# Attention with normalised queries and keys, then a SoLU layer: a new order of work for the first five groups of heads

## The chip, the cores and the metric

The kernel runs on one core of a Trainium2 chip. The metric is the device time of one execution in microseconds (us), the median of several runs. Times of single instructions come from one profiled execution, whose own time is given beside them. The engines are named as the profile names them: PE is the matrix engine (PEld its weight loads), DVE the vector engine, ACT the scalar engine, POOL the general engine (GpSimd), SP the engine that issues most of the transfers. Each runs its own list of instructions in order.

## The reference

Inputs are q, k and v of shape (8, 12, 448, 64), that is 96 heads of 448 rows and 64 columns, two gains of 64 values, and the weights of a feed-forward layer.

```python
q_n, k_n = (rmsnorm(q, g_q), rmsnorm(k, g_k))      # x / sqrt(mean(x*x) + 1e-6) * g
scores = 1.0 / np.sqrt(64) * np.matmul(q_n, k_n.transpose(0, 1, 3, 2))
attn = np.exp(scores - max); attn = attn / (sum + 1e-09)
x = np.matmul(attn, v)                             # laid out as 3584 tokens x 768
h = x @ w_in                                       # 768 x 1024
solu = h * softmax(h)
out = layernorm(solu, g_ln) @ w_out                # 1024 x 768
```

All of it is in 32-bit floats.

## The kernel before

**Stages.** Attention comes first (up to some 330 us of the profile), then the first product and the SoLU and norm of the feed-forward layer, then the second product. Both products are done by a scheme of seven block products. The change touches the attention only; what follows takes its input from a DRAM buffer `xd` that the attention writes, and its instructions are not changed.

**Quads and pairs.** Attention walks over 24 quads of four heads, `for m in range(NQ)`. A quad is two pairs of heads, `a = 2m` and `b = 2m + 1`. One pair's q and k fill a tile of 128 partitions by 896 values: each 32x32 block of q or k lies so that a transpose inside 32x32 blocks turns it into `qkT`, which has two heads' 64 columns on the partitions and the 448 positions along the free axis.

**Preparing a pair.** In the order in which one needs the other:

- `squares(n)` (line 662, ACT) squares the pair's q and k.
- `row_sums(n)` (line 670, DVE) sums each group of 32 values.
- `fold_sums(m)` (lines 680 and 681, POOL) adds for a whole quad the two halves of each row, which lie on different partitions: four copies of 32 partitions by 56 values, then one addition. `fold_one(n)` (lines 690 and 691, DVE) does the same for one pair, with four copies by 28 values and an addition.
- `rsqrt_seed` (lines 700 and 701, ACT) and `rsqrt_step` (lines 707 to 710, DVE) make one over the root mean square, for whatever width they are given.
- `normalise(n)` (line 719, POOL) multiplies the pair's q and k by it.
- `qk_transpose(n)` (line 729, DVE) makes `qkT`, and `gain(n)` (line 733, ACT) multiplies its q half by the product of both gains and 1/8.

Quad 0 is loaded in another layout and prepared by functions of its own (`square_rows`, `sum_rows`, `normalise_rows`, `transpose_rows`, `take_rows`, lines 738 to 794), with PE transposes.

**Attention of a quad.** `scores(n, kc)` (line 818, PE) makes the scores of one pair for 128 keys, kc = 0 to 2, and right after it ACT takes the exponential into a tile `E` (line 808). `scores_last(m)` (line 831) makes the last 64 keys of both pairs in one tile, so a quad has seven such tiles. They come from three PSUM buffers (tag "t"), which also serve the column sums `sm`. `add(n)` (line 845, DVE) adds `E` 0 and 1 of a pair into `es`. `add_more(n)` (line 854) adds `E` 2 to it, on POOL, or on DVE in the last two quads, for pairs of which `whole(n)` is true. `values_last` and `values` (lines 864 and 875, PE) multiply by v. `sums(m)` (line 897, PE) adds up the columns by products with ones: one term for the last tile, one for each `es`, and one for `E` 2 of each pair that is not whole; a term is four products, which the profile counts as eight instructions. `inverse(m)` (lines 908 to 916) takes the reciprocal, and `divide(m)` (lines 923 and 924, DVE) scales the outputs and so frees their two PSUM buffers. `store_x(m)` (line 932, SP) writes them to `xd`.

**Order.** The loop runs inside a manual schedule: each engine gets its instructions in the order in which the Python calls are made. `unit(f)` calls f and then whatever `later` has put off until that point; `later(1, divide)` at the end of a quad places `divide` after the next quad's first scores.

```python
def whole(n):
    return on_vector(n // 2) or n > 9 and n % 2 < 1
```

Quad 0 has a sequence of its own, ended by `continue`. In it each pair of quad 1 gets its own norm (`norms["one", n]`), and the squares and row sums of quad 2 follow late. From quad 1 on, `early = 3 < m and next1` separates two orders. In quads 4 to 22 (`early`) the norms of the next quad open the quad, its pair a is transposed after the first scores and pair b after the sixth. In quads 1 to 3 these calls sit at other places, a different one in each quad, and `divide` and `store_x` of quads 1 and 2 are made in the middle of the next quad's scores. `scarce = m < 5` also places `squares(b + 4)` and `add(b)` differently in quads 1 to 4.

**Loads.** `load(m)` issues eight transfers from SP (line 636). Quads 1 to 3 are loaded before the loop, quad 4 at the start of quad 1, and from then on quad m + 3 in quad m. Tiles of q and k have four buffers, those of v two.

Of the kernel before, what the change touches and what calls it, by code (L numbers as in the profile page):

```python
# [366 lines left out]
def fast_path(  # L367
# [298 lines left out]
    def row_sums(n):  # L666
        m, i = divmod(n, 2)
        if i == 0:
            norms[m] = {"part": small.tile([P, 2, 2 * NB], FP32, tag="part", name="part", bufs=2)}
        nc.vector.tensor_reduce(norms[m]["part"][:, i], st[n]["sq"], AX, OP.add)  # L670
# [9 lines left out]
            e.tensor_copy(ss[g * 32 : g * 32 + 32], part[o * 32 : o * 32 + 32])  # L680
        e.tensor_tensor(ss, ss, part, OP.add)

    def fold_one(n):

        m, i = divmod(n, 2)
        ss = small.tile([P, 4 * NB], FP32, tag="ss", name="ss", bufs=2)[:, 0 : 2 * NB]
        part = norms[m]["part"][:, i]
        for g in range(4):
            o = g ^ 1
            nc.vector.tensor_copy(ss[g * 32 : g * 32 + 32], part[o * 32 : o * 32 + 32])  # L690
        nc.vector.tensor_tensor(ss, ss, part, OP.add)
        norms["one", n] = {"ss": ss}

    def rsqrt_seed(d):
        ss = d["ss"]
        p, w = ss.shape
        y = d["y"] = small.tile([P, 4 * NB], FP32, tag="ny", name="ny", bufs=2)[0:p, 0:w]
        nc.scalar.activation(y, ss, AF.Ln, scale=1.0 / D, bias=eps[0:p])  # L700
        nc.scalar.activation(y, y, AF.Exp, scale=-0.5)

    def rsqrt_step(d):
        y, ss = d["y"], d["ss"]
        p, w = ss.shape
        x = small.tile([P, 4 * NB], FP32, tag="nx", name="nx", bufs=2)[0:p, 0:w]
        nc.vector.tensor_scalar(x, ss, -0.5 / D, -0.5e-6, OP.mult, OP.add)
        nc.vector.tensor_tensor(x, x, y, OP.mult)
        nc.vector.tensor_tensor(x, x, y, OP.mult)
        nc.vector.scalar_tensor_tensor(y, x, 1.5, y, OP.add, OP.mult)  # L710

    def normalise(n, e=nc.gpsimd):
        d = st[n]
        if ("one", n) in norms:
            y = norms["one", n]["y"]
        else:
            y = norms[n // 2]["y"][:, n % 2 * 2 * NB : (n % 2 + 1) * 2 * NB]
        d["qkn"] = work.tile([P, 2 * NB, 32], FP32, tag="qkn", name="qkn", bufs=2)
        e.tensor_tensor(  # L719
            d["qkn"].rearrange("p (s b) d -> p s b d", s=2),  # L720
            d["qk"].rearrange("p s (b d) -> p s b d", d=32),
            y.rearrange("p (s b) -> p s b ()", s=2).to_broadcast([P, 2, NB, 32]),
            OP.mult,
        )
# [6 lines left out]
    def gain(n):  # L731
        d = st[n]
        nc.scalar.activation(d["qkT"][:, 0], d["qkT"][:, 0], AF.Copy, scale=gcol[:, KF : KF + 1])
# [105 lines left out]
    def on_vector(m):  # L839
        return m >= NQ - 2  # L840

    def add(n):
        d = st[n]
        d["es"] = work.tile([P, 2, S], FP32, tag="es", name="es")
        nc.vector.tensor_tensor(d["es"], d["E", 0], d["E", 1], OP.add)  # L845

    def whole(n):
        return on_vector(n // 2) or n > 9 and n % 2 < 1

    def add_more(n):  # L850
        d = st[n]
# [518 lines left out]
    with tc.manual_schedule():  # L1370
# [19 lines left out]
        for m in range(NQ):  # L1390
            a, b = 2 * m, 2 * m + 1

            def outputs():
                values_last(m)
                values(a)


            next1 = m + 1 < NQ
            next2 = m + 2 < NQ
            next3 = m + 3 < NQ  # L1400
            if m == 0:
                unit(lambda: scores(a, 0))
                normalise_rows(1, 0)
                normalise_rows(1, 1)
                unit(lambda: scores(a, 1))
                unit(lambda: scores(a, 2))
                for s in range(2):
                    transpose_rows(1, s)
                    take_rows(1, s)
                squares(2)  # L1410
                add(a)
                row_sums(2)
                fold_one(2)
                unit(lambda: scores_last(m))
                squares(3)
                rsqrt_seed(norms["one", 2])
                rsqrt_step(norms["one", 2])
                normalise(2)
                unit(lambda: scores(b, 0))
                row_sums(3)  # L1420
                fold_one(3)
                unit(lambda: scores(b, 1))
                unit(lambda: scores(b, 2))
                rsqrt_seed(norms["one", 3])
                rsqrt_step(norms["one", 3])
                normalise(3)
                qk_transpose(2)
                gain(2)
                add(b)
                unit(outputs)  # L1430
                squares(4)
                qk_transpose(3)
                gain(3)
                unit(lambda: values(b))
                squares(5)
                unit(lambda: sums(m))
                inverse(m)
                row_sums(4)
                row_sums(5)
                fold_sums(2)  # L1440
                later(1, lambda m=m: divide(m))
                continue
            early = 3 < m and next1
            def norms_next():
                rsqrt_seed(norms[m + 1])
                rsqrt_step(norms[m + 1])
                normalise(a + 2)
                normalise(b + 2)

            if early:  # L1450
                norms_next()
            for x in joins_at.get(m, ()):
                combine_in(x)
            if next1:
                load_v(m + 1)
            if m == 1:
                load(m + 3)
            unit(lambda: scores(a, 0))
            if m not in (2, 3):
                store_x(m - 1)  # L1460
            if early:
                qk_transpose(a + 2)
                if next3:
                    load(m + 3)
            if m == 3:
                norms_next()
                divide(m - 1)
                store_x(m - 1)
            unit(lambda: scores(a, 1))
            if m == 2:  # L1470
                norms_next()
                divide(m - 1)
                store_x(m - 1)
            unit(lambda: scores(a, 2))
            if m == 3:
                qk_transpose(a + 2)
                load(m + 3)
            unit(lambda: scores_last(m))
            if m == 3:
                norm_gain()  # L1480
            if m < 2:
                add(a)
            unit(lambda: scores(b, 0))
            if m == 1:
                norms_next()
            if m == 2:
                qk_transpose(a + 2)
                load(m + 3)
            unit(lambda: scores(b, 1))
            if early or 1 < m < 4:  # L1490
                qk_transpose(b + 2)
            if m > 1:
                add(a)
                if not on_vector(m):
                    add_more(a)
            unit(lambda: scores(b, 2))
            if m == 1:
                qk_transpose(a + 2)
            scarce = m < 5
            if next2:  # L1500
                squares(a + 4)
                if not scarce:
                    squares(b + 4)
                row_sums(a + 4)
            if next1:
                gain(a + 2)
            if m == 1:
                add(b)
                qk_transpose(b + 2)
                squares(b + 4)  # L1510
            if next1:
                gain(b + 2)
            if scarce and m > 1:
                squares(b + 4)
                add(b)
            if next2:
                row_sums(b + 4)
                fold_sums(m + 2)
            if not scarce:
                add(b)  # L1520
            if on_vector(m):
                add_more(a)
                add_more(b)
            unit(outputs)
            step(m - 2)
            begin(m)
            step(m - 1)
            if m - 1 in sets:
                load_next()
            if m == 2:  # L1530
                load_next()
                load_next()
            unit(lambda: values(b))
            if m == NQ - 1:
                block_sums(0, 0)
                block_sums(0, 1)
                load_x(1)
            unit(lambda: sums(m))
            inverse(m)
            if next1 and m not in (1, 2):  # L1540
                later(1, lambda m=m: divide(m))
            if m == NQ - 2:
                load_x(0)
                sizes(0)
# [188 lines left out]
```

## Time and profile before

| what | value |
|---|---|
| runs | 809.93 us median of 3 (808.85 to 811.12) |
| the profiled execution | 809.46 us, its span 807.7 us |
| PE busy | 793.2 us, 98% of the span |
| DVE, POOL, ACT busy | 615.4, 505.7 and 474.0 us |
| chain that ended last | PE 91%, DVE 4%, ACT 1%, DMA 1%, POOL 1%, issue 1% |
| scores, values, column sums | lines 818, 875, 897 |

The span is the time from the first to the last instruction of the profiled execution; the rest of its own time lies around it. A busy share of PE of 98% does not say that nothing is to be had: matrix instructions overlap, so that small gaps hide in the sum. The chain, read in order of time, shows where PE was waiting for another engine: there it leaves PE's lines and passes through the others.

### The profile page before, as it was taken

What the parts mean: (1) busy time and instruction counts of PE and PEld (TensorE: products, weight loads), DVE (VectorE), ACT (ScalarE), POOL (GpSimd) and SP (SyncE); (2) the same over time, 40 slices, a digit from 0 to 9 for tenths busy, and PEclk for the clock granted to TensorE, in tenths of its full rate; (3) what the DMA queues carried; (4) which work ended last, traced back from release to release, by engine and by line L of the source; (5) the groups of instructions that cost most, each with busy time, mean ns of one, the idle gap of its engine ahead of it and who ended that gap; (6) DMA issues with size and microseconds to landing.
All of it is one profiled execution on the core that took longest, in us unless ns stands there. A gap on an engine that the chain in (4) does not pass through costs nothing.

```text
span 807.7 us, 14348 instructions
## 1 busy us (share of the span) xinstructions
PE 793.2 (98%) x4894; PEld 466.1 (58%) x4894; DVE 615.4 (76%) x1217; ACT 474.0 (59%) x785; POOL 505.7 (63%) x652
## 2 busy tenths in 40 slices
PE   8999999999999999999999999999899999999997
PEld 4334444444434444444444444444699999999996
DVE  6877889889888897488878667776886776866945
ACT  6677878778787774466766544453515455464420
POOL 1353677777777685234456466678487777777861
PEclk9999999999999999999999999999999999999999
DMA  9867798988877833545555445542647447365412
GB/s 164 176 149 150 166 191 191 190 180 175 172 155 165 155 97 97 139 122 153 153 135 138 110 108 144 140 116 52 209 119 256 144 176 267 117 227 192 141 60 83
DMA packets 269598, 122.68 MB, mean 152 GB/s; under 512 B 187596, under 2 KB 254668, under 8 KB 269516
## 3 DMA queue, kind: packets, MB, share of 16 engines
q1 hardware_dynamic: 254332, 111.78, 55.6%
q10 hardware_dynamic: 15184, 9.90, 4.5%
q8 instruction: 40, 0.66, 0.4%
q14 instruction: 42, 0.34, 0.1%
HBM read 84.94 MB, written 36.70 MB: 151 GB/s over the span
## 4 chain that ended last, share of the span: by engine, by line
PE 91%; DVE 4%; ACT 1%; DMA 1%; POOL 1%; issue 1%; SPq 0%; DVEq 0%; POOLq 0%; ACTq 0%
PE A L1210 15%; PE o L875 13%; PE s L818 13%; PE A L996 13%; PE B L996 8%; PE B L1210 7%; PE sm L897 5%; PE C L996 4%; PE D L996 4%; PE C L1210 4%; PE o L864 2%; PE s L831 2%; DMA ur<-ud 1%; ACT E L808 1%; DVE ub L1100 1%
## 5 line engine op out<-in xcount | busy, mean ns | idle before, releaser
L808 ACT ACTIVATE E<-s 128x896 f32<-128x896 f32 x168 | 139.1, 934 | 13.7 <-PE s L818 13.0
L818 PE MATMUL s<-qkT 64*64 64x448 f32 x1152 | 120.3, 545 | 1.4 <-ACT E L808 0.7
L875 PE MATMUL o<-E,v 128*64 128x448 f32 x576 | 113.5, 543 | 0.0
L1085 POOL TENSOR_TENSOR he<-he,mhalf 128x1 f32<-128x1 f32 x28 | 27.6, 987 | 105.4 <-DVE he L1084 104.9
L719 POOL TENSOR_TENSOR qkn<-qk,ny 128x896 f32<-128x896 f32 x46 | 77.2, 1698 | 21.1 <-DMA qk<-in_k_dram 15.1
L1210 PE MATMUL B<-w_out,sums 128*128 128x192 f32 x392 | 80.4, 328 | 2.8 <-DVE P L1272 2.1
L818 PEld LDWEIGHTS s<-qkT 64*64 64x64 f32 x1152 | 48.1, 163 | 59.3 <-ACT E L808 28.9
L1210 PE MATMUL A<-w_out,sums 128*128 128x192 f32 x392 | 80.7, 329 | 1.0 <-POOL sums L1191 0.7
L875 PEld LDWEIGHTS o<-E,v 128*64 128x64 f32 x576 | 39.2, 137 | 72.6 <-issue 67.3
L996 PE MATMUL B<-w_in,xsum 128*128 128x512 f32 x168 | 76.7, 593 | 0.4 <-POOL he L1085 0.4
L996 PE MATMUL A<-w_in,xg 128*128 128x512 f32 x168 | 74.6, 593 | 0.0
L1067 ACT ACTIVATE u<-h,hmax 128x1024 f32<-128x1024 f32 x28 | 32.1, 1148 | 62.9 <-DVE hmax L1061 62.8
L1210 PEld LDWEIGHTS B<-w_out,sums 128*128 128x128 f32 x392 | 66.8, 191 | 3.4 <-DVE P L1272 2.4
L1210 PEld LDWEIGHTS A<-w_out,sums 128*128 128x128 f32 x392 | 66.8, 191 | 1.7 <-POOL sums L1191 1.6
L680 POOL COPY ss<-part 32x56 f32<-32x56 f32 x88 | 42.0, 477 | 25.4 <-DVE part L670 21.0
L996 PEld LDWEIGHTS B<-w_in,xsum 128*128 128x128 f32 x168 | 31.8, 190 | 40.9 <-issue 38.5
L996 PEld LDWEIGHTS A<-w_in,xg 128*128 128x128 f32 x168 | 31.8, 190 | 40.1 <-issue 39.6
L854 POOL TENSOR_TENSOR es<-es,E 128x896 f32<-128x896 f32 x17 | 35.9, 2110 | 30.4 <-ACT sq L662 30.4
L845 DVE TENSOR_TENSOR es<-E 128x896 f32<-128x896 f32 x48 | 53.2, 1110 | 0.5 <-ACT E L808 0.5
L729 DVE STREAM_TRANSPOSE qkT<-qkn 128x896 f32<-128x896 f32 x46 | 48.5, 1089 | 1.8 <-POOL qkn L719 1.8
L670 DVE TENSOR_REDUCE part<-sq 128x28 f32<-128x896 f32 x46 | 48.2, 1078 | 2.2
L1210 PE MATMUL A<-w_out,s 128*128 128x192 f32 x224 | 45.6, 326 | 0.0
(152 smaller groups left out, 1658.0 us busy)
## 6 DMA issues: line engine op xcount, KB each, us to landing
ur<-ud SPq DMA_DIRECT2D x60, 256.0 KB, 4.9
ud<-ub SPq DMA_DIRECT2D x112, 128.0 KB, 2.3
xd<-xo SPq DMA_DIRECT2D x48, 224.0 KB, 3.0
qk<-in_q_dram SPq DMA_DIRECT2D x92, 112.0 KB, 3.1
qk<-in_k_dram SPq DMA_DIRECT2D x92, 112.0 KB, 3.0
v<-in_v_dram SPq DMA_DIRECT2D x24, 384.0 KB, 4.5
out_dram<-P SPq DMA_DIRECT2D x19, 384.0 KB, 4.0
raw<-in_moe_w_in_dram SPq DMA_DIRECT2D x12, 512.0 KB, 5.3
```

The costliest lines, as they stand in the source:

```text
L670: nc.vector.tensor_reduce(norms[m]["part"][:, i], st[n]["sq"], AX, OP.add)
L680: e.tensor_copy(ss[g * 32 : g * 32 + 32], part[o * 32 : o * 32 + 32])
L719: e.tensor_tensor(d["qkn"].rearrange("p (s b) d -> p s b d", s=2), d["qk"].rearrange("p s (b d) -> p s b d", d=32), y.rearrange("p (s b) - ...
L729: nc.vector.transpose(d["qkT"].rearrange("p s t -> p (s t)"), d["qkn"].rearrange("p b d -> p (b d)"))
L808: nc.scalar.activation(d["E", kc], s[:, :, 0:S], AF.Exp)
L818: nc.tensor.matmul(s[c : c + D, h, 0:S], d["qkT"][hh, 1, keys], d["qkT"][hh, 0, :], start=True, stop=True,)
L845: nc.vector.tensor_tensor(d["es"], d["E", 0], d["E", 1], OP.add)
L854: e.tensor_tensor(d["es"], d["es"], d["E", 2], OP.add)
L875: nc.tensor.matmul(d["o"][h * D : (h + 1) * D, :], quads[n // 2]["v"][:, n % 2 + 2 * h, kc], d["E", kc][:, h], start=False, stop=(kc == NJ ...
L897: nc.tensor.matmul(sm[g : g + 32, :], ones[:, w], e[:, h, t * S // 2 : (t + 1) * S // 2], start=(x == 0), stop=(x == len(terms) - 1),)
L996: nc.tensor.matmul(k[bank], a[:, c], w_in[i][:, c], start=begin and c == 0, stop=c == HD - 1, skip_group_check=not begin,)
L1210: nc.tensor.matmul(k[bank], a[:, c].rearrange("p a i -> p (a i)"), w_out[:, area, i, c], start=begin and c == 0, stop=c == KC - 1, skip_gr ...
```

## The change

Five things are done to the order of the attention, and one term of the column sums moves to POOL.

- **Quad 0.** `fold_one` is gone. The squares and row sums of pairs 2 and 3 are followed by one `fold_sums(1)` on POOL and one `norms_next()` for both pairs. `add(b)` comes earlier, ahead of those norms. `squares(4)`, `row_sums(4)` and `squares(5)` stand ahead of the transpose of pair 2, `row_sums(5)` between the two transposes, and `fold_sums(2)` after the second. `gain(3)` leaves the quad.
- **Quad 1** gets `gain(3)` after its first scores.
- **Quads 1 to 4** take the order of the later ones: norms of the next quad first, transposes after the first and the sixth scores, `add` and `squares` where the later quads have them, `divide` and `store_x` by `later` in all of them.
- **g's turn.** The transpose of the norm gain `g_ln` (`norm_gain`) in quad 3 moves from the middle of the scores to between the values of both pairs.
- **Column sums.** `whole(n)` is true for every even n. In quads 0 to 4, `E` 2 of pair a is added by POOL (`add_more`), and the column sums have four terms in place of five.

```diff
-    def fold_one(n):
-        m, i = divmod(n, 2)
-        ss = small.tile([P, 4 * NB], FP32, tag="ss", name="ss", bufs=2)[:, 0 : 2 * NB]
-        ...
-        norms["one", n] = {"ss": ss}
...
     def whole(n):
-        return on_vector(n // 2) or n > 9 and n % 2 < 1
+        return on_vector(n // 2) or n % 2 == 0
...
+            early = m > 0 and next1
+
+            def norms_next():
+                rsqrt_seed(norms[m + 1])
+                rsqrt_step(norms[m + 1])
+                normalise(a + 2)
+                normalise(b + 2)
...
                 squares(2)
                 add(a)
+                add_more(a)
                 row_sums(2)
-                fold_one(2)
                 unit(lambda: scores_last(m))
                 squares(3)
-                rsqrt_seed(norms["one", 2])
-                rsqrt_step(norms["one", 2])
-                normalise(2)
                 unit(lambda: scores(b, 0))
                 row_sums(3)
-                fold_one(3)
+                fold_sums(1)
                 unit(lambda: scores(b, 1))
                 unit(lambda: scores(b, 2))
-                rsqrt_seed(norms["one", 3])
-                rsqrt_step(norms["one", 3])
-                normalise(3)
+                add(b)
+                norms_next()
+                squares(4)
+                row_sums(4)
+                squares(5)
+                unit(outputs)
                 qk_transpose(2)
                 gain(2)
-                add(b)
-                unit(outputs)
-                squares(4)
+                row_sums(5)
                 qk_transpose(3)
-                gain(3)
+                fold_sums(2)
                 unit(lambda: values(b))
-                squares(5)
                 unit(lambda: sums(m))
                 inverse(m)
-                row_sums(4)
-                row_sums(5)
-                fold_sums(2)
                 later(1, lambda m=m: divide(m))
                 continue
-            early = 3 < m and next1
...
             unit(lambda: scores(a, 0))
-            if m not in (2, 3):
-                store_x(m - 1)
+            if m == 1:
+                gain(3)
+            store_x(m - 1)
             if early:
                 qk_transpose(a + 2)
-                if next3:
+                if next3 and m > 1:
                     load(m + 3)
-            if m == 3:
-                norms_next()
-                divide(m - 1)
-                store_x(m - 1)
             unit(lambda: scores(a, 1))
-            if m == 2:
-                norms_next()
-                divide(m - 1)
-                store_x(m - 1)
             unit(lambda: scores(a, 2))
...
             unit(lambda: scores_last(m))
-            if m == 3:
-                norm_gain()
-            if m < 2:
-                add(a)
             unit(lambda: scores(b, 0))
-            if m == 1:
-                norms_next()
...
             unit(lambda: scores(b, 1))
-            if early or 1 < m < 4:
+            if early:
                 qk_transpose(b + 2)
-            if m > 1:
-                add(a)
-                if not on_vector(m):
-                    add_more(a)
+            add(a)
+            if not on_vector(m):
+                add_more(a)
             unit(lambda: scores(b, 2))
...
             if next2:
                 squares(a + 4)
-                if not scarce:
-                    squares(b + 4)
+                squares(b + 4)
                 row_sums(a + 4)
             if next1:
                 gain(a + 2)
                 gain(b + 2)
             if next2:
                 row_sums(b + 4)
                 fold_sums(m + 2)
-            if not scarce:
-                add(b)
+            add(b)
...
+            if m == 3:
+                norm_gain()
             unit(lambda: values(b))
...
-            if next1 and m not in (1, 2):
+            if next1:
                 later(1, lambda m=m: divide(m))
```

More of the change, by code (lines that the diff above doesn't have):

```diff
@@ L681, in fold_sums @@
         e.tensor_tensor(ss, ss, part, OP.add)
-    def fold_one(n):
-        m, i = divmod(n, 2)
-        ss = small.tile([P, 4 * NB], FP32, tag="ss", name="ss", bufs=2)[:, 0 : 2 * NB]
[L687 to L691, printed above, removed]
-        norms["one", n] = {"ss": ss}
     def rsqrt_seed(d):
@@ L713, in normalise @@
         d = st[n]
[L714 to L717, printed above, removed]
+        y = norms[n // 2]["y"][:, n % 2 * 2 * NB : (n % 2 + 1) * 2 * NB]
         d["qkn"] = work.tile([P, 2 * NB, 32], FP32, tag="qkn", name="qkn", bufs=2)
@@ L1411, in fast_path @@
                 add(a)
+                add_more(a)
                 row_sums(2)
-                fold_one(2)
                 unit(lambda: scores_last(m))
                 squares(3)
-                rsqrt_seed(norms["one", 2])
-                rsqrt_step(norms["one", 2])
-                normalise(2)
                 unit(lambda: scores(b, 0))
                 row_sums(3)
-                fold_one(3)
+                fold_sums(1)
                 unit(lambda: scores(b, 1))
                 unit(lambda: scores(b, 2))
-                rsqrt_seed(norms["one", 3])
-                rsqrt_step(norms["one", 3])
-                normalise(3)
+                add(b)
[4 more added lines that the diff above has]
+                unit(outputs)
                 qk_transpose(2)
                 gain(2)
-                add(b)
-                unit(outputs)
-                squares(4)
+                row_sums(5)
                 qk_transpose(3)
-                gain(3)
+                fold_sums(2)
                 unit(lambda: values(b))
-                squares(5)
                 unit(lambda: sums(m))
                 inverse(m)
-                row_sums(4)
-                row_sums(5)
-                fold_sums(2)
                 later(1, lambda m=m: divide(m))
                 continue
-            early = 3 < m and next1
[L1444 to L1448, printed above, removed]
             if early:
@@ L1458, in fast_path @@
             unit(lambda: scores(a, 0))
-            if m not in (2, 3):
-                store_x(m - 1)
+            if m == 1:
+                gain(3)
+            store_x(m - 1)
             if early:
                 qk_transpose(a + 2)
-                if next3:
+                if next3 and m > 1:
                     load(m + 3)
-            if m == 3:
-                norms_next()
-                divide(m - 1)
-                store_x(m - 1)
             unit(lambda: scores(a, 1))
-            if m == 2:
-                norms_next()
-                divide(m - 1)
-                store_x(m - 1)
             unit(lambda: scores(a, 2))
-            if m == 3:
-                qk_transpose(a + 2)
-                load(m + 3)
             unit(lambda: scores_last(m))
-            if m == 3:
-                norm_gain()
-            if m < 2:
-                add(a)
             unit(lambda: scores(b, 0))
-            if m == 1:
-                norms_next()
-            if m == 2:
-                qk_transpose(a + 2)
-                load(m + 3)
             unit(lambda: scores(b, 1))
-            if early or 1 < m < 4:
+            if early:
                 qk_transpose(b + 2)
-            if m > 1:
-                add(a)
-                if not on_vector(m):
-                    add_more(a)
+            add(a)
+            if not on_vector(m):
+                add_more(a)
             unit(lambda: scores(b, 2))
-            if m == 1:
-                qk_transpose(a + 2)
-            scarce = m < 5
             if next2:
                 squares(a + 4)
-                if not scarce:
-                    squares(b + 4)
+                squares(b + 4)
                 row_sums(a + 4)
@@ L1506, in fast_path @@
                 gain(a + 2)
-            if m == 1:
-                add(b)
-                qk_transpose(b + 2)
-                squares(b + 4)
-            if next1:
                 gain(b + 2)
-            if scarce and m > 1:
-                squares(b + 4)
-                add(b)
             if next2:
@@ L1518, in fast_path @@
                 fold_sums(m + 2)
-            if not scarce:
-                add(b)
+            add(b)
             if on_vector(m):
```

## The prediction

> **What bounds the kernel.** I read the chain that ended last first, then its first 110 us in order of time, then the timelines of DVE, ACT and POOL over quad 0. Over the whole span the chain says:
>
> ```profile
> PE 91%; DVE 4%; ACT 1%; DMA 1%; POOL 1%; issue 1%; SPq 0%; DVEq 0%; POOLq 0%; ACTq 0%
> ```
>
> Time is won only where this chain leaves PE or where PE does less. The chain in order of time (start, duration, what) shows both, from the transposes of pair 2 to the start of quad 6:
>
> ```profile
> 26.70 0.67 ACT qkT L733
> 27.37 0.84 ACT sq L662
> 28.21 0.81 ACT E L808
> ...
> 37.91 2.03 PE sm L897 x40
> 39.94 0.99 PE s L818 x8
> 40.93 0.02 issue
> 40.95 1.73 ACT E L808 x2
> 42.68 0.24 ACT ny L700
> ...
> 54.21 0.99 PE s L818 x8
> ...
> 56.74 0.60 issue
> 57.35 0.92 ACT E L808
> 58.27 0.04 issue
> 58.31 2.57 PE s L818 x24
> ...
> 68.33 2.45 PE s L818 x24
> ...
> 81.22 2.45 PE s L818 x24
> ...
> 92.09 1.65 PE sm L897 x32
> 93.74 2.45 PE s L818 x24
> ```
>
> The first scores of quads 2 to 6 start at 39.94, 54.21, 68.33, 81.22 and 93.74, so quads 2, 3, 4 and 5 last 14.27, 14.12, 12.89 and 12.52 us. Quad 5 is PE without a gap and has 32 products of column sums; quad 4 has 40, and quads 2 and 3 also leave PE for ACT's exponentials, behind which stand ACT's norms (line 700) and, in quad 3, the norm gain.
>
> **The skill.** The Trainium skill, "SBUF — State Buffer", section "Who interferes with whom", says that a DVE instruction with two SBUF inputs and a GpSimd instruction that reads SBUF exclude each other for the whole instruction, and that a reduction on trn2 never collides. The trace agrees. In quad 0:
>
> ```profile
> 23.86 1.78 DVE L845 TENSOR_TENSOR es<-E 128x896 f32<-128x896 f32 x1
> 23.00 1.70 POOL L719 TENSOR_TENSOR qkn<-qk,ny 128x896 f32<-128x896 f32 x1 [2.16 <-DVE ny L710]
> 18.97 1.08 DVE L670 TENSOR_REDUCE part<-sq 128x28 f32<-128x896 f32 x1
> 91.08 2.59 POOL L680 COPY ss<-part 32x56 f32<-32x56 f32 x4
> ```
>
> The addition lasts 1.78 us against 1.08 elsewhere: it ran only once POOL had finished at 24.70. The reduction beside an earlier multiplication of POOL (19.14 to 20.84) was not held. In quad 5 the four copies took 2.59 us, beside an addition at 90.87, against 1.02 us alone. "Perfetto Trace Analysis", section "Identifying the Most-Contended Engine", warns that the matrix engine's busy share is no measure of what it has left; the trace agrees, as slices with PE at 100% hold the slow quads above.
>
> **Quads 2 to 4.** They get the order and the sums of quad 5. Their work on POOL is then two multiplications (3.4 us), one `add_more` (2.1), the fold (1.3) and the reciprocals' copies (0.9): 7.7 of 12.5 us, as in quad 5, which on top has a weight conversion. The price of each quad is taken from quad 5:
>
> 3 x 12.52 = 37.56 against 14.27 + 14.12 + 12.89 = 41.28: 3.72 us less.
>
> The norm gain moves to between the values of quad 3. Its transpose took 0.22 us; its copy on ACT (0.18) falls where ACT is idle. I put 0.1 us back: 3.6 less. The five fewer terms of sums are each 2.03 - 1.65 = 0.38 us; those of quads 2 to 4 are in this 3.72, those of quads 0 and 1 below. SP's order (v, store, q and k, weights) is the same as before in each of these quads, only its times are earlier, and from 40 to 48 us the transfers were almost idle.
>
> **Quads 0 and 1.** Here I follow the chain by hand, with about 0.05 us for each handover. Before, the first scores of quad 1 start at 26.21, held by the sums, which waited for `add(b)` (0.46 us idle on PE).
>
> - PE: values end at 23.5, as before. The sums have one term less and `add(b)` is early: PE is free at 25.2.
> - The squares of pair 3 end at 17.71, then follow three exponentials without the norm between them: 17.75 to 20.2. `row_sums(3)` is done at 18.8.
> - `add_more(0)` on POOL: 15.9 to 18.0, beside reductions, hidden. The fold of quad 1 could run from 18.9 to 20.2, but `add(b)` (DVE, ready with the second exponential at 19.4) collides with it: I take 1.0 us more, its end at 21.25.
> - Seed on ACT 21.3 to 21.9, steps on DVE (four of 0.2) to 22.65, multiplications on POOL 22.7 to 24.4 and 24.4 to 26.1.
> - `squares(4)` on ACT from 21.95. It needs quad 2's q and k: the last of their transfers is issued before 17.83, and that group took 2.9 to 4.5 us to land, so 20.3 to 21.8: just in time. `row_sums(4)` to 24.0, ahead of the transpose.
> - Transpose of pair 2: 24.5 to 25.55. Gain to 26.25. First scores of quad 1 at 26.3 against 26.21: PE's 1.0 us is lost to this wait.
> - `row_sums(5)` to 26.5, transpose of pair 3 to 27.6, then `inverse` (28.3). The fold of quad 2 on POOL: 26.6 to 28.0, so ACT's seed, which now stands ahead of every exponential of quad 1, ends at 28.65, and the first exponential starts then, against 28.11.
> - `gain(3)` follows it (0.65), ahead of the second exponential. The last scores wait for it and start at 30.15 against 29.06; ACT sets the pace until the seventh exponential ends at 35.1 (before: 34.3). The values of quad 1 start at 33.45 against 32.50. `divide(0)` ends at 32.1, ahead of that.
> - 0.75 + 4.66 + 1.65 brings quad 2 to 40.5 against 39.94: 0.5 us more. Its own seed is ready by 41.2 and delays nothing; its pairs are transposed by 34.3.
>
> Bounds: if the collision costs nothing, the fold is 1.0 sooner, but `row_sums(4)` then holds the transpose, and quad 2 starts at about 39.9 (0.0). At best PE runs without a gap from 25.2: 25.2 + 12.52 = 37.7 (2.2 us less). At worst the collision costs the 1.6 us of quad 5 and the squares start 0.5 late: 1.5 us more.
>
> Sum: 3.6 - 0.5 = 3.1 us less. Against the profiled execution that is 809.46 - 3.1 = 806.4; against the median 809.93 - 3.1 = 806.8. I forecast 806.6. The rest of the attention and the later stages have the same instructions and follow in order, so the shift carries to the end; the waits there (573 to 586 us, DVE and the `ur` transfers) hang on PE's own progress.
>
> **Rivals.**
>
> 1. *The opening flows better.* PE starts quad 1 near 25.2 and ACT never holds it: 2.2 us less in place of 0.5 more, 803.6 to 805.5. For it: DVE and POOL have idle stretches before 23 us, and the collision is an assumption. Against it: the seed of quad 2 on ACT needs the fold, which needs the transposes. Chance 0.13.
> 2. *The opening loses most of it.* One fold in place of two short ones on DVE makes both pairs of quad 1 wait for the later, and ACT's first exponential stands behind squares, gain and seed. Costs of 1.2 to 4 us leave 0 to 2.4 of gain: 807.5 to 810. For it: the pair's fold on DVE cost 0.9 us, the quad's on POOL 1.3 and more. Chance 0.17.
> 3. *Slower: quad 2's load holds ACT.* `squares(4)` was issued at 24.55 and now at 21.95, ahead of the gain of pair 2, the seed and every exponential of quad 1. From a landing at t the first scores follow at t + 0.95 + 1.05 + 1.1 + 0.65 and handovers, about t + 3.85, so past 22.45 each us late is a us lost; the gain is gone at 25.6, and at 28 the kernel is 0.3% slower, 812.5. For it: transfers at 0.8 to 1.1 of the engines' share from 2 to 34 us. Against it: the landing times above. Chance 0.06.
> 4. *Nothing changes.* The gaps in quads 2 and 3 come from PE and ACT's pace and stay: 809 to 810. Against it: quads 5 and 6 have as many exponentials and no gap. Chance 0.04.
>
> **How the numbers follow.** What a measurement can tell from no change is 0.3%, 2.4 us: below 807.5 is faster. My own case has 0.60, of which 0.06 lies between 807.5 and 808. With rival 1 that makes 0.67 for faster; same is 0.06 + 0.15 + 0.04 = 0.25 (0.02 of rival 2 falls beyond); slower 0.08. The range runs from 804.8, which leaves out part of rival 1, to 808.6, which takes in half of rival 2 and leaves out the worse half, rivals 3 and 4.
>
> **What the changed profile would show.** First scores of quad 2 near 40.5, those of quads 3, 4, 5 12.5 us apart, `sm` always x32, and no ACT line in the chain from 43 us on. ACT's seed of quad 2 ending near 28.6, ahead of quad 1's first exponential. The four copies of quad 1's fold longer than 1.02 us beside `add(b)`. A `squares(4)` that starts well past 22 would be rival 3. I am wrong if quad 2 starts past 43, or if quads 2 to 4 are longer than 13 us each.

## The result, and the profile after

The changed kernel takes 806.78 us (median of 7 runs, 805.87 to 807.20) against 809.74 (7 runs, 808.85 to 811.12): ratio 0.9961, 95% interval 0.9950 to 0.9972. Run again beside the first experiments, on a chip where the kernel before took 809.44 us, it took 807.88 us (21 runs): ratio 0.9976, 0.9969 to 0.9982. So the change wins 0.2 to 0.5%, 1.5 to 4 us; the forecast was 3.1. The profiled execution took 807.2 us, with a span of 805.4 (before: 809.46 and 807.7).

The chain that ended last, over the whole span:

```profile
PE 88%; DVE 3%; DMA 2%; SPq 2%; POOL 2%; ACT 1%; issue 1%; DVEq 0%; ACTq 0%; POOLq 0%
```

PE has less of it than before (91%), though the kernel is faster. The chain in order of time shows where (start, duration, what; in the changed kernel's lines 802 and 815 are the scores, 859 the values, 881 the column sums, 687 and 688 the seed, 792 the exponential):

```profile
25.19 1.05 DVE part L670
...
27.80 0.35 ACT ny L687
28.17 0.25 ACT ny L688
28.42 0.81 ACT E L792
...
29.28 1.53 PE s L815 x8
...
40.33 2.45 PE s L802 x24
...
52.85 2.45 PE s L802 x24
...
61.46 0.15 PE pg L476
...
65.67 2.45 PE s L802 x24
...
76.54 1.65 PE sm L881 x32
78.19 2.45 PE s L802 x24
```

From 29.28 on the attention's chain is PE alone up to the first scores of quad 21 (278.48), and the sums have 32 products. The opening is ruled by POOL, DVE and ACT, up to the seed that stands ahead of quad 1's first exponential. (Ahead of POOL's multiplication at 22.45 the chain passes through a transfer of q and k and SP's issues. But POOL starts 0.08 us after DVE's last step of the norm ended at 22.35, and 0.08 us after it in the repeated run as well, so the norm is the likelier release.) Quad by quad, with the first scores of quad 0 at 10.70 before and 10.46 after:

| first scores of | before | after | a quad lasts, before and after |
|---|---|---|---|
| quad 2 | 39.94 | 40.33 | 14.27, 12.52 |
| quad 3 | 54.21 | 52.85 | 14.12, 12.82 |
| quad 4 | 68.33 | 65.67 | 12.89, 12.52 |
| quad 5 | 81.22 | 78.19 | 12.52, 12.52 |

At quad 5 the kernel is 3.03 us ahead, and 0.24 of that is the earlier opening. It keeps that up to the first scores of the last quad (in PE's timeline 303.18 against 306.22), but the next stage's first products start at 316.42 after 318.46, only 2.04 us earlier. The chain says where a microsecond went, before and then after:

```profile
306.29 2.45 PE s L818 x24
308.74 0.75 PE s L831 x8
```

```profile
296.85 6.67 DMA xg<-xd
...
303.54 0.94 ACT xsum L941 x2
...
305.45 0.81 ACT E L792
...
306.30 0.98 PE s L815 x8
```

`xg` is the first input tile of the feed-forward layer. Its sums of squares (`sizes(0)`, line 941) stand on ACT ahead of the exponentials of the last quad, and wait for the transfer. The timelines of ACT, before and then after:

```profile
305.58 0.84 ACT L957 ACTIVATE xsum<-xg 128x768 f32<-128x768 f32 x1 [3.66 <-DMA xg<-xd]
```

```profile
303.54 0.84 ACT L941 ACTIVATE xsum<-xg 128x768 f32<-128x768 f32 x1 [4.67 <-DMA xg<-xd]
```

ACT waited in both kernels. Before, the transfer landed 5.65 us after its issue (299.88 to 305.53) and PE never noticed; now it took 6.67 (296.85 to 303.52), and PE stood still for 0.6 us ahead of the last scores and worked at ACT's pace behind them.

### The profile page after: what moved, and what is told of

Its sections match the earlier page's. It is cut to its first block, busy times and chain, and to the rows that moved or that the text cites. A ratio compares the mean times of both kernels' runs of the same rounds, so it can differ in the third digit from the quotient of the medians.

```text
span 805.4 us, 14271 instructions
## 1 busy us (share of the span) xinstructions
PE 789.7 (98%) x4854; PEld 464.5 (58%) x4854; DVE 612.8 (76%) x1203; ACT 473.0 (59%) x783; POOL 519.9 (65%) x662
## 4 chain that ended last, share of the span: by engine, by line
PE 88%; DVE 3%; DMA 2%; SPq 2%; POOL 2%; ACT 1%; issue 1%; DVEq 0%; ACTq 0%; POOLq 0%
PE A L1194 15%; PE A L980 13%; PE o L859 12%; PE s L802 12%; PE B L980 8%; PE B L1194 8%; PE C L980 4%; PE sm L881 4%; PE D L980 4%; PE C L1194 4%; PE s L815 2%; PE o L848 2%; SPq L636 1%; DMA ur<-ud 1%; DMA xg<-xd 1%
## 5 line engine op out<-in xcount | busy, mean ns | idle before, releaser
L838 POOL TENSOR_TENSOR es<-es,E 128x896 f32<-128x896 f32 x22 | 46.4, 2109 | 48.9 <-ACT sq L662 35.4
L680 POOL COPY ss<-part 32x56 f32<-32x56 f32 x92 | 46.8, 508 | 6.7 <-DVE part L670 2.2
```

The costliest lines, as they stand in the source:

```text
L838: e.tensor_tensor(d["es"], d["es"], d["E", 2], OP.add)
```

## The experiments

A word ahead on how profiles are compared. In some executions PE is granted half its clock for a stretch near 585 us, and in others not; the windows of the kernel before, from 587.0 to 590.5 us (busy time of PE, weight loads, DVE, ACT and POOL, then the granted clock, the transfers' share and GB/s):

```profile
587.00:590.50 3.50, 3.50 (x13) 3.50 (x12) 1.57 (x6) 0.00 (x0) 3.42 (x5) 0.52 0.94 241
```

In such a window PE does the work of 1.8 us at full clock: 1.7 us are lost. The mean grant from 580 to 600 us is 0.91 in the profiles of before and after, and 1.00 in five of the others. So I compare profiles by their stages up to 320 us and not by their spans, and times by their medians.

**The change again.** No edit.

> The changed kernel again, as the yardstick for the others and for one reading of its profile: there quad 5 starts 3.03 us earlier than before, but the last stage only 2.04 us earlier, because ACT waits 4.67 us for the first transfer of the next stage (xg), 6.67 us in landing against 5.65. Theory: this is chance of a transfer whose cover is used up, so in another execution the landing is again between 5.6 and 6.7 us, PE loses what it exceeds about 6.1 us by, and the time lies between 805.8 and 807.3. Rival: it is a fixed cost of the earlier end of the attention; then the landing is 6.6 us or more again and PE is held 0.6 us or more at the last quad's seventh tile.

807.88 us, ratio 0.9976. Quad 5 starts at 78.35, the next stage at 316.90. The transfer took 6.99 us (297.01 to 304.00) and PE waited 0.9 us for ACT there. The landing is thus no accident of one execution: the time is above what the first theory gave, and the rival's numbers came. Its reason, the earlier end of the attention, does not hold: the column sums alone, below, end it later and have the late landing too.

**The column sums alone.**

```diff
 # the kernel before
-        return on_vector(n // 2) or n > 9 and n % 2 < 1
+        return on_vector(n // 2) or n % 2 == 0
...                          # quad 0, and the same in quad 1
                 add(a)
+                add_more(a)
```

> The kernel before with the column sums of the change alone: POOL adds the third exponential of pair a in quads 0 to 3 too, and quads 0 to 4 have four terms; nothing else moves. Theory: five terms of 0.38 us are 1.9 us, but the addition on POOL (2.1 us, from 15.9 us) now holds [...]the copies of pair 2's norm on DVE in quad 0 (16.8 us in the old order), which delays quad 1 by about 1 us; in quad 1 it also holds the norm's steps, hidden. So 0.5 to 1.2 us less than before, 808.5 to 809.2, with quads 2 and 3 still longer than 13.5 us each. Rival: the terms come off in full wherever they stand; then 1.9 us less, 807.8.

812.36 us, ratio 1.0041 (1.0027 to 1.0054): slower, by 3 us. Both theories fell on the size, mine even on the sign. The collisions that I expected are there, in the timelines of POOL and DVE:

```profile
15.85 2.09 POOL L854 TENSOR_TENSOR es<-es,E 128x896 f32<-128x896 f32 x1 [8.89 <-DVE es L845]
```

```profile
16.73 1.80 DVE L690 COPY ss<-part 32x28 f32<-32x28 f32 x4
...
34.55 1.59 DVE L708 TENSOR_TENSOR nx<-nx,ny 128x56 f32<-128x56 f32 x1 [0.62 <-ACT ny L701]
```

The copies take 1.80 us against 0.72 before, and in quad 1 a step of the norm takes 1.59 against 0.22, behind POOL's addition (33.98 to 36.07). What I called hidden there was not: this step is in the chain that ended last, behind it pair 4's transposes and the fold of quad 3 (at 43.65, against 40.81 before), for which ACT's seed waits among quad 2's exponentials. And quad 1 was hit a second time. The windows of this kernel:

```profile
23.00:27.00 4.00, 2.10 (x36) 0.83 (x32) 3.68 (x6) 1.73 (x3) 1.70 (x1) 1.00 1.03 161
27.00:31.50 4.50, 4.50 (x36) 1.76 (x32) 4.43 (x7) 3.28 (x5) 1.71 (x9) 0.62 0.99 206
```

PE was busy for 2.10 of 4.00 us, with one wait of 1.90 us for `es`, and then had 0.62 of its clock: quad 1's 24 score instructions took 4.19 us against 2.45 elsewhere. The Trainium skill, "TensorE: Matmul & The Clock Gate", section "What's actually happening", says that an idle window of about 3.4 us, free-running, puts PE at half its clock. The profile agrees on the half and on the length (0.62 over 4.5 us is 3.4 us at half clock); but PE was half busy here, and not idle. Here the wait was followed by a loss of 1.74 us, almost its own length once more; the waits of 0.5 to 1.2 us at `xg` were followed by none (grant 1.00 from 300 to 320 us in all profiles). Of the 3 us, 1.66 are there at the first scores of quad 5, and 0.93 come in the last quad, where `xg` took 6.60 us and held ACT here too. In the old order this part of the change is a loss; in the new one it is a gain, as the next run shows.

**The order alone.**

```diff
 # the changed kernel
-        return on_vector(n // 2) or n % 2 == 0
+        return on_vector(n // 2) or n > 9 and n % 2 < 1
```

> The changed kernel with the old column sums (five terms in quads 0 to 4, POOL adds nothing in quads 0 to 4). Theory: quads 1 to 4 pay 0.38 us each, 1.5 us; quad 0's term stays hidden, because PE waits for pair 2's gain there anyway. So 1.5 us more than the change, 808.3, and quads 2 and 4 last 12.9 us. Rival: the order is the whole gain and the terms are hidden behind ACT; then no more than 0.5 us, 807.3.

808.36 us, ratio 0.9990 (0.9982 to 0.9999), beside 0.9976 for the whole change on the same chip. The chain of its profile, at the entry of quad 2:

```profile
38.85 2.03 PE sm L881 x40
40.88 2.45 PE s L802 x24
```

Quads 2 to 5 start at 40.88, 53.78, 66.98 and 79.88. Quads 2, 3 and 4 last 12.90, 13.20 and 12.90 us, each 0.38 more than in the change, and quad 5 starts 1.53 us later than in the change run beside it: four terms of 0.38, and nothing for quad 0's, as expected. Against the kernel before, the order alone is 1.34 us ahead at quad 5 (81.22 to 79.88) and the change 2.87 (81.22 to 78.35), so the order makes somewhat less than half of the gain there and the shorter sums the rest. Of the 1.53 us the next stage sees 0.42 (317.32 against 316.90), because here `xg` landed in 5.9 us and PE lost some 0.2 us at the end in place of 1.3. The loss at the end eats most of what the sums win by then.

**The new first quad alone.**

```diff
 # the changed kernel's quad 0, and gain(3) after the first scores of quad 1; else as before:
+            early = 3 < m and next1
+        return on_vector(n // 2) or n == 0 or n > 9 and n % 2 < 1
```

> The new quad 0 (with its four-term sums, and the third pair's gain in quad 1), but quads 1 to 4 in the old order with the old sums. Theory: the new first quad wins nothing by itself, PE is held at the first scores of quad 1 as before; what is left is that the seed of quad 2 no longer waits ahead of quad 1's exponentials. So 0 to 0.8 us less than before, 809 to 809.7, quads 2 and 3 at 14 us each. Rival: the first quad is where the gain lies; then 2 us less or more, 807.7 or below.

809.25 us, ratio 1.0002 (0.9995 to 1.0009). Quad 2 starts at 39.61 (39.94 before; the openings differ by 0.16), quads 2 and 3 last 14.27 and 14.12 us. The new first quad wins nothing by itself.

**The old first quad under the new order.**

```diff
 # the changed kernel, with quad 0 and fold_one of the kernel before
-        return on_vector(n // 2) or n % 2 == 0
+        return on_vector(n // 2) or n > 0 and n % 2 == 0
...
-            if m == 1:
-                gain(3)
```

> The old quad 0 (two norms on DVE, squares and row sums of quad 2 last, five terms of sums) with the new order in quads 1 to 4. Theory: quads 2 to 4 keep their 12.5 to 12.8 us, but the seed of quad 2, now ahead of every exponential of quad 1 on ACT, waits for a fold that ends at 30.8 us in the old quad 0 (27.8 in the new one), so quad 1's last scores come about 3 us later than in the change and quad 2 starts near 43 in place of 40.4. So 2 to 3 us more than the change, about 809.5 to 810.5 where the change has 807.5. Rival: the first quad's layout is worth nothing; then the time is that of the change within 0.5 us.

810.44 us, ratio 1.0011 (1.0003 to 1.0019): slower than before, and some 3 us above the change by the ratios. But in its profile the grant is 0.79 from 9 to 17 us, ahead of all that was edited, and quad 1 begins 1.6 us late for that alone. So it was run once more.

> The old first quad under the new order once more, because its first profile had a stretch of half clock at 11 to 15 us, before anything that was changed, which put all of quad 0 back by 1.6 us. Theory: that stretch is chance and is missing here; the fold of quad 2 then ends near 30.8 us, PE waits 3.5 us for the seed and the exponential behind it, and a stretch of half clock follows that wait again; quad 2 starts near 44.4. Rival: the stretch behind the wait was chance as well; then quad 2 starts near 42.8.

809.89 us, ratio 1.0004 (0.9996 to 1.0013). The chain of this run, the longest of PE's waits, and the windows behind it:

```profile
30.69 0.35 ACT ny L700
31.06 0.25 ACT ny L701
31.31 0.81 ACT E L808
...
32.17 1.77 PE s L831 x8
33.94 4.16 PE s L818 x24
```

```profile
PE s L831 <- ACT E L808: 3.6, 1, 3.6
```

```profile
9.00:17.00 8.00, 7.33 (x66) 3.86 (x68) 6.36 (x14) 7.09 (x13) 0.00 (x0) 1.00 1.06 193
32.00:37.00 5.00, 4.83 (x28) 1.78 (x32) 4.90 (x8) 3.57 (x6) 3.35 (x2) 0.50 0.61 106
```

The stretch in the opening is missing here; one behind the wait came in both profiles. The seed waits for a late fold, every exponential of quad 1 waits for the seed, PE stands 3.56 us, and then works at half clock: the last scores take 1.77 us and pair b's 4.16. In the first profile the half clock came later behind the same wait (grant 0.66 from 34 to 39 us), and they took 0.98 and 4.04; pair b's take 2.45 at full clock. Here the grant was 0.50 for all 5 us from 32 to 37, longer than the 3.4 us of half clock found in the sums alone. Quad 2 starts at 45.16, later than the first theory had it. Yet quads 2 to 4 last 12.52, 12.82 and 12.52 us: the order keeps its gain there. So the parts hang together: the order and the shorter sums of quads 1 to 4 make the gain, and the new first quad pays its entry.

**The norm gain back among the scores.**

```diff
 # the changed kernel
             unit(lambda: scores_last(m))
+            if m == 3:
+                norm_gain()
...
-            if m == 3:
-                norm_gain()
```

> The changed kernel with the norm gain's transpose back in the middle of quad 3's scores. Theory: in its new place it costs 0.30 us (quad 3 lasts 12.82 against 12.52); in the old one it takes a PSUM buffer between two scores and makes PE wait for ACT, 0.6 to 0.9 us in all. So 0.3 to 0.6 us more than the change, too little for the runs but to be seen in the profile as a quad 3 of 13.1 to 13.4 us. Rival: it is what made quad 3 slow before; then 1.2 us or more.

807.38 us, ratio 0.9973 (0.9964 to 0.9981), not to be told from the change. Quad 3 lasts 13.24 us (53.11 to 66.35) against 12.82: 0.42 us more, inside what was expected. In the new place it costs 0.30.

**The sums of squares late.**

```diff
 # the changed kernel
             if on_vector(m):
                 add_more(a)
                 add_more(b)
+            if m == NQ - 1:
+                sizes(0)
...
             if m == NQ - 2:
                 load_x(0)
-                sizes(0)
```

> The changed kernel with the sums of squares of the next stage's first tile (sizes(0), two ACT instructions that wait for the xg transfer) put behind the last quad's exponentials. Theory: in the change they hold ACT at the start of the last quad, because the transfer lands 6.7 to 7.0 us after its issue, and PE is held 1.0 to 1.4 us; behind the exponentials they wait for nothing. So 1.0 us less than the change, and the last stage starts 3.0 us earlier than before. Rival: the next stage's first products then wait for them or for POOL's sums behind them; then no gain.

805.52 us, ratio 0.9954 (0.9941 to 0.9968). ACT's timeline and PE's chain at the last quad:

```profile
304.44 5.77 ACT L792 ACTIVATE E<-s 128x896 f32<-128x896 f32 x7 [5.38 <-PE s L802]
310.03 0.91 ACT L941 ACTIVATE xsum<-xg 128x768 f32<-128x768 f32 x1
```

```profile
303.42 2.45 PE s L802 x24
305.87 0.75 PE s L815 x8
```

The transfer was no sooner (7.3 us), but PE has no gap in the last quad any more. The next stage starts at 315.56, with the opening at 10.64: 2.84 us ahead of before when both are counted from their first scores, against 1.80 in the change. The loss at the end is this wait.

**The same in the kernel before.** The same edit, in the kernel before.

> The kernel before with the same move of sizes(0) behind the last quad's exponentials. Theory: before, the xg transfer landed 5.65 us after its issue, just inside the cover that the last quad's first scores give, so the move wins nothing: the time of the kernel before within 0.5 us. Then what the change lost at the end of the attention came with the change. Rival: the move is a gain of its own of 1 us in any kernel.

808.94 us, ratio 0.9991 (0.9982 to 0.9999). From the first scores of quad 0 the next stage comes after 307.72 us (10.49 to 318.21), against 307.76 before: nothing, as the first theory said. The loss at the end came with the change.

**The seed behind the first exponential.**

```diff
 # the changed kernel
-            if early:
+            if early and m > 1:
                 norms_next()
...
-            unit(lambda: scores(a, 0))
-            if m == 1:
-                gain(3)
+            unit(lambda: (scores(a, 0), gain(3), norms_next()) if m == 1 else scores(a, 0))
```

> The changed kernel with the seed of quad 2's norm on ACT behind the first exponential and the gain of quad 1 (and not ahead of every exponential). Theory: ACT idles 1.83 us there, from 25.95 to 27.80, waiting for the fold, while the first scores of quad 1 are done at 26.9; the exponential then starts 1.4 us earlier and quad 2 starts about 0.9 us earlier, near 39.4. So 0.9 us less than the change. Rival: something else holds quad 1's last scores (pair 3's transpose and gain); then 0.3 us or less.

806.90 us, ratio 0.9961 (0.9947 to 0.9976), beside 0.9973 for the kernel of the norm gain. From quad 1's first scores to quad 2's it takes 13.71 us (26.28 to 39.99) against 14.31 in the change: 0.6 us less, between the two expectations. The first exponential starts 1.08 us after PE begins those scores in place of 2.3, but the second still stands behind the gain and the seed and starts at 29.25 (29.68 in the change).

**`add(b)` apart from the fold.**

```diff
 # the changed kernel
     def rsqrt_step(d, between=None):
...
         nc.vector.tensor_scalar(x, ss, -0.5 / D, -0.5e-6, OP.mult, OP.add)
+        if between:
+            between()
...
-                rsqrt_step(norms[m + 1])
+                rsqrt_step(norms[m + 1], (lambda: add(b)) if m == 0 else None)
...
-                add(b)
                 norms_next()
```

> The changed kernel with add(b) of quad 0 placed behind the fold, between the first and the second step of the norm, so that DVE's addition and POOL's four copies don't meet. Theory: the copies then take 1.02 us in place of 1.83, the seed comes 0.8 us sooner, the addition fills DVE's wait for it, and quad 1's first scores start about 0.4 us sooner (near 25.6 in place of 26.0, the transfers of quad 2 allowing). So 0.4 us less than the change, to be seen in the profile and hardly in the runs. Rival: squares(4) then waits for the load of quad 2 and the transpose for its row sums; then nothing.

807.09 us, ratio 0.9966 (0.9953 to 0.9979). POOL's timeline, in the change and then here:

```profile
18.73 1.83 POOL L680 COPY ss<-part 32x56 f32<-32x56 f32 x4 [0.92 <-DVE part L670]
```

```profile
18.82 1.01 POOL L680 COPY ss<-part 32x56 f32<-32x56 f32 x4 [0.93 <-DVE part L670]
```

The collision cost 0.8 us on POOL. Quad 1's first scores start 15.19 us after those of quad 0, against 15.56: 0.37 us, as expected. The rest of the 0.8 is lost on DVE, where the addition outlasts the seed:

```profile
20.36 1.08 DVE L831 TENSOR_TENSOR es<-E 128x896 f32<-128x896 f32 x1
```

The seed ends at 20.88, but the steps of the norm start at 21.36 (21.60 and 21.63 in the change). ACT's squares of quad 2 now wait 0.64 us, which the profile puts down to a transfer; that held nothing up, as DVE's transpose waited for POOL (to 23.86) and not for the row sums (done at 23.59).

**All three.** The last three edits of the changed kernel (sums of squares late, seed behind, `add(b)` apart) together.

> The changed kernel with all three moves: sizes(0) late, the seed of quad 2 behind the first exponential, add(b) apart from the fold. Theory: they lie on different stretches of the chain and add up, 1.1 + 0.6 + 0.4 us less than the change, so 4.5 to 5.3 us less than before (0.9940). Rival: the two in quads 0 and 1 share one wait; then 0.3 us or less beyond the late sizes alone.

805.65 us, ratio 0.9954 (0.9940 to 0.9969), the same as with the late sums of squares alone. In the profile they do add up: quad 2 starts 28.92 us after the first scores of quad 0 (29.87 in the change), and the next stage at 314.59, 0.97 us before that of the late sums of squares. The medians, taken on different chips, don't show this microsecond; the profile here had the stretch of half clock (grant 0.62 from 583.0 to 587.2 us), that of the late sums of squares had none (1.00 from 580 to 600). Whether that is where it went in the timed runs stays open. Both versions are faster than the kernel before. Against the change their ratios are lower (0.9954 beside 0.9961 and 0.9976), but the intervals touch, so the gain over the change is shown by the profiles' stages and not by the times.

## Why the prediction was right, and where it was off

- **Quads 2 to 4, "3.72 us less", "3.6" with the norm gain.** Right: 41.28 - 37.86 = 3.42. The quads are those of quad 5 to the hundredth; the term that was mis-sized is the norm gain in its new place, put at 0.1 and measured at 0.30.
- **The terms of 0.38 us.** Right, as the order alone shows for four of them. That quad 0's is lost to a wait was right as well.
- **Quads 0 and 1, "0.5 us more".** Measured 0.39, or 0.63 from each kernel's own first scores. The points on the way: first scores of quad 1 at 26.02 (26.3 forecast), the seed's end at 28.42 (28.65), the last scores at 29.28 (30.15), quad 2 at 40.33 (40.5). The last scores started sooner because only their second half, that of pair b, waits for `gain(3)`; they took 1.53 us for that. The collision of `add(b)` with the fold, assumed at 1.0 us, cost 0.8. The 2.59 us of quad 5, from which the worst case of 1.6 was taken, were not the addition's alone: two steps of the weight conversion on DVE (91.88 to 93.31) stood beside those copies as well, and quad 0 has none.
- **"The rest follows in order, so the shift carries to the end."** This is the step that failed. It carried to the first scores of the last quad; then 1.0 us was lost where ACT waits for `xg`. The trace of before shows that wait of 3.66 us on ACT, and I did not ask how near it stood to PE: the last scores of the last quad came some 0.4 us after ACT's first exponential had ended. A transfer that lands 1.0 us later is enough. The forecast was met because this loss and the runs' spread are smaller than the range. That the first medians differ by 2.96 us, so close to the forecast of 3.1, is luck: the profiles give 2.04 at the next stage, of which 0.24 is the opening, which the change does not touch, and the repeated run gives 1.56.
- **Rival 3 (quad 2's load).** Not so: `squares(4)` started at 21.67, directly behind the seed. But it was close: in the repeated run it started at 22.13, 0.39 us behind the seed, and the prediction reckoned a loss from 22.45 on.
- **Left open: why `xg` lands later.** The kernel before (with the sums of squares in either place), the order alone, the new first quad alone and the old first quad have it in 5.1 to 5.9 us in their profiles; the change, those built on it with its sums in all of quads 0 to 4, and the sums alone have it in 6.6 to 7.3. It seems to go with the kernel and not with the execution (the change and the old first quad have two profiles each, the others one), and not with the time of issue: the sums alone issue it at 301.9 us and have it late, the order alone at 298.5 and have it early. The cause was not tried.

## What to carry to other kernels

A wait that costs nothing is a distance, not a zero: for each engine in front of the bound one, note how much later it may become, the transfers ahead of it too, because a shift elsewhere can use that up. An order that works in the steady state needs its entry built for it: here the order without the new opening was no faster than the kernel before (ratios 1.0011 and 1.0004), and the moved additions without either were slower (1.0041). An instruction that waits for a transfer belongs behind the work that feeds the bound engine, as long as its own reader is late.

## What the runs showed of the hardware

- In the attention, long waits on PE were followed by a stretch of half clock and short ones were not: PE busy for 2.10 of 4.00 us with a wait of 1.90, then a grant of 0.62 over 4.5 us (the sums alone); a wait of 3.6 us, then 0.66 over 5 us in one profile of the old first quad and 0.50 over 5 us in the other. Such a stretch cost 1.6 to 2.5 us on top of the wait. Behind waits of 0.5 to 1.2 us at the last quad the grant stayed at 1.00. A stretch also came without such a wait, from 11 to 15 us in one of the two profiles of the old first quad.
- Near 585 us such a stretch stands in nine of the fourteen profiles and not in the other five, at up to 1.7 us each, as much as the smaller effects of this study. PE's longest wait there is 2.1 us in the kernel before, with a stretch, and 2.2 us in the late sums of squares, without one, so a wait of this length does not decide it.
- A transfer of 768 KB between the same buffers took 5.1 to 5.9 us in one group of kernels and 6.6 to 7.3 in another, with only the two stores of 224 KB ahead of it still in flight.
